# Six tokens of every head on 96 partitions: another layout for k and v of two batches in a fused linear-attention and SwiGLU kernel

## The chip, the cores and the metric

The kernel runs on one core of a Trainium2 chip. The metric is the device time of one execution in microseconds (us). Three timed executions of the kernel before gave 323.48, 323.53 and 322.88 us, so its median is 323.48 us.

A core has a tensor engine (PE, with its weight loads listed apart as PEld), a vector engine (DVE), a scalar engine (ACT), a general engine (POOL, in the code `gpsimd` or `G`), a sync engine (SP) that here only issues transfers, and 16 DMA engines that carry the transfers of all queues. Each engine runs its own instructions in order and waits on semaphores for the others.

## The reference

The inputs are q, k and v of 8 batches, 8 heads, 576 tokens and 64 channels, and the weights of a feed-forward layer. All are float32; the kernel computes its products in bfloat16.

```
phi(x) = concat(relu(x) * cos(theta_s), relu(x) * sin(theta_s))    # 64 -> 128 features, theta_s = pi/2 * s/576
kv  = einsum('bhsf,bhsd->bhfd', phi(k), v)        # per batch and head 128 x 64, a sum over the 576 tokens
z   = sum over s of phi(k)                         # 128
num = phi(q) @ kv ;  den = phi(q) @ z + 1e-6
x   = num / den, heads side by side                # 4608 tokens x 512
xn  = x / sqrt(mean(x^2) + 1e-6) * rms_g
out = (silu(xn @ w_gate) * (xn @ w_val)) @ w_out   # 512 -> 1536 -> 512
```

kv and z of a head are one product here: v gets a 65th column of ones, and phi(k) (128 features, stationary) times that v (65 columns, moving) is accumulated over chunks of tokens into one 128 x 65 piece of the PSUM tile `psA`.

## The kernel before

**How the work is tiled.** The feed-forward part works on nine blocks: block b holds 512 tokens of batch b, and block 8 holds the last 64 tokens of all batches. In each block 12 steps make the hidden tile `hT` (gate product, value product, silu on ACT, multiplication on DVE), and four output steps multiply it with `w_out` and store. The attention of batch b + 1 is put between the steps of block b and the first steps of block b + 1, so that PE always has a large product to run. The order of all instructions is written out by hand: `at(block, step, where, function, ...)` (line 753) files small pieces of work into slots, and `run` (line 756) emits them. Nothing reorders them afterwards.

**k and v, and how a batch comes in.** For the sum over tokens any assignment of tokens to partitions is allowed, as long as k, v and the cos/sin table agree. Two layouts are in use before.

- Batches 0, 1 and 2 are narrow: two heads share the 128 partitions, 64 partitions each, and a partition holds 9 consecutive tokens of one head in each of 4 head pairs. `kv_rows` (line 70) describes it; a load has 512 pieces of 2,304 bytes. Each product has 64 rows: the even head on partitions 0 to 63 and the odd head on 64 to 127, so one batch takes 4 pairs x 9 chunks x 2 = 72 products (line 394).
- Batches 3 to 7 are wide (`wide`, line 75): a partition holds 5 consecutive tokens of every head, on 116 partitions (576 = 5 x 115 + 1). A load has pieces of 1,280 bytes and goes in two parts, 112 partitions and the rest. One batch takes 8 heads x 5 chunks = 40 products of 115 or 116 rows (line 387).

A batch needs, in order: the loads of k and v into buffers of a ring (tag `raw`, 5 buffers), `k_phi` (cos half on DVE, sin half on ACT, one instruction for each chunk and half), `v_cast` (to bfloat16 beside the column of ones), `kvz_pe` (the products), `kvz_evac` (ACT copies psA to SBUF), and then four times `nd_pe` and `nd_post` (phi(q) times kv, and the division).

**The start and its POOL queue.** Batch 0 has no large products to hide behind. SP loads its k at once. POOL first writes the token indices with five `iota` instructions (lines 158 to 162; 20 columns of indices, from which DVE and ACT make the cos/sin table `tab`), then issues through its own DMA queue, in this order: half of q of batch 0, v of batch 0 (cast on the way into a tile of its own, `vv0`, line 210), the rest of q, four loads of gate and value weights, k of batch 1 (line 228), gate weights for steps 8 to 11, and later, between other POOL work, value weights for steps 8 to 11, q of batch 1, v of batch 1 (line 699), three loads of `w_out`, k of batch 2 and v of batch 2 (lines 772 and 775). Two POOL memsets at lines 274 and 275 set the columns of ones of two tiles, `vv` for narrow batches and `vv5` for wide ones.

**Batches 1 and 2.** `k_phi` of batch 1 follows units 5, 6 and 7 of block 0, three chunks at a time (line 762). Its `v_cast` is split: POOL casts the first two head pairs (line 773, at step 9) and DVE the last two (line 774, at step 10). POOL issues v of batch 2 behind its cast. `kvz_pe(1)` stands in `last_step` (line 801), between the gate and the value product of step 11. `k_phi` of batch 2 is spread 3, 2, 2 and 2 chunks over four places (line 824, `KCS`), its cast runs on DVE in two halves, and `kvz_pe(2)` comes before step 3 of block 1 (line 839).

Of the kernel before, what the change touches and what calls it, by code (L numbers as in the profile page):

```python
# [9 lines left out]
FP32 = mybir.dt.float32  # L10
# [7 lines left out]
def kernel(  # L18
# [15 lines left out]
    P = 128  # L34
# [3 lines left out]
    NC5 = 5  # L38
    KP = S // NC5 + 1
    KM = 112  # L40
    NDT = DM // P
    NNT = DFF // P
    E = D + 1
# [26 lines left out]
    def kv_rows(src, b, hps):  # L70
        return src[b, 2 * hps[0] : 2 * hps[1], :, :].rearrange(
            "(hp hh) (s c) d -> (hh s) hp (c d)", hh=2, c=NC
        )

    def wide(b):
        return b > 2

    def rows_of(c):
        return KP if c == 0 else KP - 1

    def kv_rows5(src, b, r0, r1):
# [9 lines left out]

    def raw_tile(which, b):
        if (which, b) not in raw:
            t = ring.tile([P, H * NC5 * D], FP32, name="raw", tag="raw")
            raw[(which, b)] = t
        return raw[(which, b)]

    def raw_kv(which, b):
        t = raw_tile(which, b)
        if wide(b):  # L100
            return t[:, :].rearrange("p (h e) -> p h e", h=H)
        return t[:, 0 : HP * NC * D].rearrange("p (hp e) -> p hp e", hp=HP)

    def raw_q(b):
# [2 lines left out]
    def load_kv(which, b, hps=(0, HP), eng=nc.sync):  # L107
        src = k if which == "k" else v
        if not wide(b):
            return eng.dma_start(  # L110
                out=raw_kv(which, b)[:, hps[0] : hps[1], :], in_=kv_rows(src, b, hps)
            )
        last = KP if b < B - 1 else KP - 1
        for r0, r1 in ((0, KM), (KM, last)):
            eng.dma_start(
                out=raw_kv(which, b)[r0:r1, :, :], in_=kv_rows5(src, b, r0, r1)
            )
        if last < KP:
            eng.dma_start(
                out=raw_kv(which, b)[last:KP, :, :].rearrange("p h (c d) -> p h c d", d=D),  # L120
                in_=src[b, :, S - 1 : S, :].rearrange("h s d -> s h d").unsqueeze(2)
                .to_broadcast([1, H, NC5, D]),
            )
# [29 lines left out]
        )  # L153


    NTAB = 20
    idx_i = one.tile([P, NTAB], mybir.dt.int32, name="idx_i")
    G.iota(idx_i[:, 0:9], pattern=[[1, 9]], base=0, channel_multiplier=9)
    G.iota(idx_i[:, 9:13], pattern=[[1, 4]], base=0, channel_multiplier=4)
    G.iota(idx_i[:, 13:14], pattern=[[0, 1]], base=512, channel_multiplier=1)  # L160
    G.iota(idx_i[:, 14:19], pattern=[[1, NC5]], base=0, channel_multiplier=NC5)
    G.iota(idx_i[:, 19:NTAB], pattern=[[0, 1]], base=NC - 1, channel_multiplier=NC)
    warm = one.tile([P, TB], BF16, name="warm")
    V.memset(warm[:, :], 0.0)
    ones = one.tile([P, P], BF16, name="ones")
# [22 lines left out]
    def load_wo(n0, n1):  # L188
        return G.dma_start(
            out=wo[:, n0:n1, :],  # L190
            in_=moe_w_out[n0 * P : n1 * P, :].rearrange("(t p) m -> p t m", p=P),
        )
# [14 lines left out]
                )  # L207
                rest = gres[:, i, :]

    vv0 = one.tile([P, HP, NC * D], BF16, name="vv0")  # L210
    load_q0(0, G)
    for hp in range(0, HP, 2):
        G.dma_start(out=vv0[:, hp : hp + 2, :], in_=kv_rows(v, 0, (hp, hp + 2)))
# [30 lines left out]
        out=th[:, 0:NTAB], in0=fidx[:, :], scalar1=S - 1.0, scalar2=ang,  # L244
        op0=ALU.min, op1=ALU.mult,
    )
    for c0, c1, i0, less in ((0, 9, 0, 576.0), (13, 14, 13, 64.0), (19, NTAB, 13, 64.0)):
        V.tensor_scalar(
            out=th[64:128, c0:c1], in0=fidx[64:128, i0 : i0 + c1 - c0],
            scalar1=-less, scalar2=ang,  # L250
            op0=ALU.add, op1=ALU.mult,
        )
# [12 lines left out]
    def cos_of(c):  # L265
        return tab[:, NTAB + c : NTAB + c + 1]

    kp5 = one.tile([P, NC5, H, F], BF16, name="kp")
    kp = kp5[:, :, :, :].rearrange("p c h f -> p (c h f)")[:, 0 : NC * HP * F].rearrange(
        "p (c hp f) -> p c hp f", c=NC, f=F  # L270
    )
    vv = one.tile([P, HP, NC, E], BF16, name="vv")
    vv5 = one.tile([P, H, NC5, E], BF16, name="vv5")
    G.memset(vv[:, :, :, D:E], 1.0)
    G.memset(vv5[:, :, :, D:E], 1.0)
    qpT = one.tile([P, H, TB], BF16, name="qpT")
    xnT = [one.tile([P, NDT, TB], BF16, name=f"xnT{i}") for i in range(2)]
    xnT_tail = one.tile([P, NDT, TB], BF16, name="xnT_tail")
# [5 lines left out]
    def copy(eng, o, i):  # L284
        if eng is A:
            A.copy(out=o, in_=i)  # L286
        else:
            eng.tensor_copy(out=o, in_=i)  # L288

    def phi(eng, out_ap, in_ap, scale):  # L290
        if eng is A:
            A.activation(out=out_ap, in_=in_ap, func=AF.Relu, scale=scale)  # L292
        else:
            eng.tensor_scalar(  # L294
                out=out_ap, in0=in_ap, scalar1=scale, scalar2=0.0, op0=ALU.mult, op1=ALU.max
            )


    def k_phi(eng, b, c, part, hps=(0, HP)):
        o = slice(0, D) if part == 0 else slice(D, F)  # L300
        f = cos_of if part == 0 else sin_of
        if wide(b):
            rows = rows_of(c)
            src = raw_kv("k", b)[0:rows, :, c * D : (c + 1) * D]
            phi(eng, kp5[0:rows, c, :, o], src, f(14 + c)[0:rows, :])
            return
        src = raw_kv("k", b)[:, hps[0] : hps[1], c * D : (c + 1) * D]
        phi(eng, kp[:, c, hps[0] : hps[1], o], src, f(c))
# [58 lines left out]
        copy(eng, qpT[:, :, j * P : (j + 1) * P], dst)  # L367

    def v_cast(eng, b, hps=(0, HP)):
        if wide(b):  # L370
            src = raw_kv("v", b).rearrange("p h (c d) -> p h c d", d=D)
            hs = slice(2 * hps[0], 2 * hps[1])
            return copy(eng, vv5[0:KP, hs, :, 0:D], src[0:KP, hs])
        copy(
            eng, vv[:, hps[0] : hps[1], :, 0:D],
            raw_kv("v", b)[:, hps[0] : hps[1], :].rearrange("p hp (c d) -> p hp c d", d=D),
        )

    heads = psA[:, :, 0 : HP * E].rearrange("p g (hp e) -> p g hp e", e=E)
    kvzs = {}  # L380

    def kvz_pe(b):
        for hp in range(HP):
            for c in range(NC5 if wide(b) else 0):
                for g in range(2):
                    h, r = 2 * hp + g, rows_of(c)
                    nc.tensor.matmul(  # L387
                        heads[:, g, hp, :], lhsT=kp5[0:r, c, h, :], rhs=vv5[0:r, h, c, :],
                        start=(c == 0), stop=(c == NC5 - 1),
                    )  # L390
            for c in range(0 if wide(b) else NC):
                for g in range(2):
                    lo, hi = 64 * g, 64 * g + 64
                    nc.tensor.matmul(  # L394
                        heads[:, g, hp, :], lhsT=kp[lo:hi, c, hp, :], rhs=vv[lo:hi, hp, c, :],
                        start=(c == 0), stop=(c == NC - 1),
                    )


# [111 lines left out]
    def x_sq(b, j):  # L511
        xt = x_of[(b, j)]
        scr = one.tile([P, DM + 1], BF16, name="scr", tag="scr")
        ms = four.tile([P, 1], FP32, name="ms", tag="ms")
        A.activation(  # L515
            out=scr[:, :], in_=xt[:, 0 : DM + 1], func=AF.Square,
            scale=1.0 / math.sqrt(DM), accum_out=ms[:, :],
        )
        rs = four.tile([P, 1], FP32, name="rs", tag="rs")
        G.tensor_tensor(out=rs[:, :], in0=ms[:, :], in1=mhalf[:, :], op=ALU.pow)  # L520
        rs_of[(b, j)] = rs
# [191 lines left out]
    x_tr_evac(V, 0, 1, psC[0])  # L713
    unit_mm(0, wv)
    x_sq(0, 2)
    load_wo(0, 4)
    unit_silu(0)
    nd0_pe(3)
# [34 lines left out]
    def at(blk, n, where, f, *args):  # L753
        slots.setdefault((blk, n), {}).setdefault(where, []).append((f, args))
# [2 lines left out]
        for f, args in slots.get((blk, n), {}).get(where, []):  # L757
            f(*args)

    KCS = ((0, 1, 2), (3, 4), (5, 6), (7, 8))  # L760
    KCS5 = ((0, 1), (2,), (3,), (4,))
    for c in range(NC):
        at(0, 5 + c // 3, "post", k_phi, V, 1, c, 0)
        at(0, 5 + c // 3, "post", k_phi, A, 1, c, 1)
    for j in range(4):
        at(0, (8, 8, 9, 10)[j], "post", q_phi, V, 1, j, 0)
        at(0, (8, 9, 10, 10)[j], "post", q_phi, A, 1, j, 1)
# [53 lines left out]
    for nb in range(2, B):  # L821
        b = nb - 1
        first = nb == 2
        for i, cs in enumerate(KCS5 if wide(nb) else KCS):
            kb, kn = ((0, 14), (0, 15), (1, 0), (1, 1))[i] if first else (b - 1, 12 + i)
            for c in cs:
                at(kb, kn, "post", k_phi, V, nb, c, 0)
                at(kb, kn, "post", k_phi, A, nb, c, 1)
        for i in range(2):
            vb, vn = ((0, 15), (1, 0))[i] if first else (b - 1, 13 + 2 * i)  # L830
            at(vb, vn, "post", v_cast, V, nb, (2 * i, 2 * i + 2))
        for j in range(4):
            late = j + (nb == 3)
            qb, qn = (b, 1 + j) if first else (b - (late < 2), (14 + late) % 16)
            at(qb, qn, "post", q_phi, V, nb, j, 0)
            at(qb, qn, "post", q_phi, A, nb, j, 1)
            at(qb, qn, "post", q_tr_dma, nb, j)
        kz = 3 if first else 2
        at(b, kz, "pe", kvz_pe, nb)
        at(b, kz, "pre", kvz_evac, A, nb)  # L840
        for j in range(4):
            n = ((6, 8, 9, 11) if first else (4, 6, 8, 10))[j]
            at(b, n, "mid" if n == 9 else "pe", nd_pe, nb, j)
            at(b, n, "pre", nd_post, nb, j)
            at(b, n, "post", x_sq, nb, j)
            m = n + 2 if first and j == 0 else n + 1
            at(b, m, "post", x_norm, nb, j)
            at(b, m, "post", x_tr_dma, nb, j)
# [110 lines left out]
```

## Time and profile before

| | us |
|---|---|
| timed executions | 322.88, 323.48, 323.53 |
| median | 323.48 |
| span of the profiled execution, first to last instruction | 321.1 |
| PE busy | 313.6 (98% of the span) |
| DVE busy | 185.4 (58%) |
| ACT busy | 165.8 (52%) |
| POOL busy | 40.5 (13%) |

The profiled execution gives its span only; its own time would lie above that by what the runtime adds before the first and after the last instruction. Against the median of the timed executions that is 323.48 - 321.1 = 2.4 us. The granted clock of PE is 1.000 over the whole span.

A busy time is the sum of an engine's instructions. The chain of waits follows the instruction that ended last back to what released it, step by step; what is on it sets the time, what is off it does not. A DMA share above 1 in a stretch means that on average more transfers were under way than the 16 engines can carry at once.

### The profile page before, as it was taken

The numbers are of one execution on the slowest core, as the hardware profiler recorded it, in microseconds if no ns is written. First come the engines' busy times: TensorE is split into PE (matmuls) and PEld (weight loads), VectorE is DVE, ScalarE is ACT, GpSimd is POOL, SyncE is SP. The second block draws the span as 40 slices with busy tenths as digits, with TensorE's granted clock in tenths as the row PEclk, the third lists the DMA queues.
The fourth block names the chain that finished last, engine by engine and source line by source line (L and its number), as shares of the span: only waits on it lengthen the run. The fifth ranks groups of instructions, "written<-read, shape, count | busy, mean of one in ns | idle before, by whom it ended". The sixth has DMA issues, their size and how long they took to land.

```text
span 321.1 us, 6023 instructions
## 1 busy us (share of the span) xinstructions
PE 313.6 (98%) x2274; PEld 162.4 (51%) x2310; DVE 185.4 (58%) x382; ACT 165.8 (52%) x322; POOL 40.5 (13%) x79
## 2 busy tenths in 40 slices
PE   7999999999999999999999999999999999999996
PEld 2689564544454445444544445544544444444444
DVE  7976977668457773777457644781676034204410
ACT  5766756754574466554744575446543233223321
POOL 9771211002001100010001100100011000000000
PEclk9999999999999999999999999999999999999999
DMA  7999999788999999999799959995522500041002
GB/s 232 239 270 269 282 329 227 201 183 190 223 226 211 187 263 187 221 247 182 162 186 230 197 163 200 197 217 163 99 59 41 116 33 0 0 102 31 1 35 98
DMA packets 80092, 53.76 MB, mean 167 GB/s; under 512 B 52235, under 2 KB 74047, under 8 KB 80063
## 3 DMA queue, kind: packets, MB, share of 16 engines
q1 hardware_dynamic: 73110, 41.25, 62.1%
q0 software_dynamic: 6944, 12.13, 15.5%
q8 instruction: 18, 0.29, 0.4%
q14 instruction: 12, 0.09, 0.1%
q10 hardware_dynamic: 8, 0.00, 0.0%
HBM read 37.83 MB, written 9.44 MB: 147 GB/s over the span
## 4 chain that ended last, share of the span: by engine, by line
PE 94%; DMA 2%; DVE 1%; issue 1%; POOL 1%; ACT 0%; POOLq 0%; ACTq 0%
PE psC L574 27%; PE psV L556 27%; PE psG L556 26%; PE psV L643 2%; PE psA L449 2%; DMA vv<-in_v_dram 2%; PE psG L574 2%; PE psG L643 2%; PE psA L387 2%; PE psA L394 1%; PE psA L474 0%; PE psV L363 0%; PE psG L430 0%; PE psC L546 0%; POOL raw L135 0%
## 5 line engine op out<-in xcount | busy, mean ns | idle before, releaser
L571 DVE TENSOR_TENSOR hT<-psV,sg 128x512 bf16<-128x512 f32 x99 | 68.2, 689 | 96.5 <-PE psV L556 64.1
L556 PE MATMUL psV<-xnT,wv 128*128 128x512 bf16 x344 | 89.6, 379 | 0.7 <-issue 0.2
L570 ACT ACTIVATE sg<-psG 128x512 f32<-128x512 f32 x99 | 58.6, 592 | 60.8 <-PE psG L556 52.7
L556 PE MATMUL psG<-xnT,wg 128*128 128x512 bf16 x337 | 88.5, 379 | 0.7 <-issue 0.2
L574 PE MATMUL psC<-wo,hT 128*128 128x512 bf16 (+1 forms) x400 | 88.4, 376 | 0.4
L574 PEld LDWEIGHTS <-hT 128*128 128x128 bf16 x456 | 43.1, 98 | 47.7
L556 PEld LDWEIGHTS <-wv 128*128 128x128 bf16 x400 | 39.0, 98 | 46.8
L556 PEld LDWEIGHTS <-wg 128*128 128x128 bf16 x400 | 37.0, 98 | 39.9 <-DVE xnT L288 0.2
L520 POOL TENSOR_TENSOR rs<-ms,mhalf 128x1 f32<-128x1 f32 x36 | 20.5, 570 | 193.9 <-ACT scr L515 193.7
L286 ACT COPY osb<-psC 128x512 f32<-128x512 f32 x32 | 18.7, 585 | 49.9 <-PE psC L574 46.1
L515 ACT ACTIVATE scr<-xt 128x513 bf16<-128x513 f32 x36 | 22.8, 635 | 23.3 <-DVE xt L499 22.3
L527 DVE SCALAR_TENSOR_TENSOR xn<-xt,rs,gb 128x512 bf16<-128x512 f32 (+1 forms) x37 | 26.9, 730 | 9.9 <-POOL rs L520 9.9
L292 ACT ACTIVATE kp<-raw,tab 128x256 bf16<-128x256 f32 (+2 forms) x51 | 28.8, 607 | 2.4 <-DMA raw<-in_k_dram 2.4
L499 DVE TENSOR_TENSOR xt<-psA,rec 128x512 f32<-128x512 f32 x36 | 24.9, 691 | 1.2
L292 ACT ACTIVATE qp<-raw,tab 128x512 bf16<-128x512 f32 (+1 forms) x36 | 23.3, 666 | 1.2 <-DMA raw<-in_q_dram 1.1
L294 DVE TENSOR_SCALAR kp<-raw,tab 128x256 bf16<-128x256 f32 (+2 forms) x53 | 20.1, 428 | 0.5 <-DMA raw<-in_k_dram 0.5
L294 DVE TENSOR_SCALAR qp<-raw,tab 128x512 bf16<-128x512 f32 (+1 forms) x34 | 15.3, 463 | 4.7 <-DMA raw<-in_q_dram 4.7
L449 PEld LDWEIGHTS <-qpT 128*128 128x128 bf16 x224 | 10.6, 97 | 6.6
L556 PE MATMUL psV<-xnT_tail,wv 128*128 128x512 bf16 x48 | 12.3, 379 | 0.1
L556 PE MATMUL psG<-xnT_tail,wg 128*128 128x512 bf16 x46 | 12.0, 379 | 0.1
L288 DVE CAST vv<-raw 116x1280 bf16<-116x1280 f32 (+1 forms) x13 | 11.1, 857 | 1.3 <-DMA raw<-in_v_dram 1.3
L449 PE MATMUL psA<-kvzs,qpT 128*128 128x65 bf16 x224 | 11.4, 193 | 0.0
(102 smaller groups left out, 177.7 us busy)
## 6 DMA issues: line engine op xcount, KB each, us to landing
out_dram<-osb SPq DMA_DIRECT2D x27, 256.0 KB, 2.3
raw<-in_q_dram SPq DMA_DIRECT2D x6, 1024.0 KB, 9.1
raw<-in_k_dram SPq DMA_DIRECT2D x5, 1120.0 KB, 8.8
raw<-in_v_dram SPq DMA_DIRECT2D x5, 1120.0 KB, 9.4
raw<-in_k_dram POOLq DMA_DIRECT2D x2, 1152.0 KB, 19.2
raw<-in_v_dram POOLq DMA_DIRECT2D x2, 1152.0 KB, 15.7
out_dram<-osb SPq DMA_DIRECT2D x17, 128.0 KB, 2.6
wg<-in_moe_w_gate_dram POOLq DMA_DIRECT2D x3, 512.0 KB, 13.8
```

Of the source, the lines that this page charges most:

```text
L286: A.copy(out=o, in_=i)
L292: A.activation(out=out_ap, in_=in_ap, func=AF.Relu, scale=scale)
L294: eng.tensor_scalar(out=out_ap, in0=in_ap, scalar1=scale, scalar2=0.0, op0=ALU.mult, op1=ALU.max)
L449: nc.tensor.matmul(heads[:, g, hp, :], lhsT=qpT[:, h, j * P : (j + 1) * P], rhs=kvzs[b][:, g, hp * E : (hp + 1) * E], start=True, stop=True,)
L499: V.tensor_tensor(out=xt[:, 0:DM].rearrange("p (hp g d) -> p g hp d", g=2, d=D), in0=heads[:, :, :, 0:D], in1=rec[:, :, :].unsqueeze(3).to ...
L515: A.activation(out=scr[:, :], in_=xt[:, 0 : DM + 1], func=AF.Square, scale=1.0 / math.sqrt(DM), accum_out=ms[:, :],)
L520: G.tensor_tensor(out=rs[:, :], in0=ms[:, :], in1=mhalf[:, :], op=ALU.pow)
L527: V.scalar_tensor_tensor(out=xn_of[(b, j)][:, c], in0=x_of[(b, j)][:, c], scalar=rs_of[(b, j)][:, :], in1=gb[:, c], op0=ALU.mult, op1=ALU. ...
L556: nc.tensor.matmul(bank[:, cols[0] : cols[1]], lhsT=w[:, t, n * P : (n + 1) * P], rhs=x[:, t, cols[0] : cols[1]], start=(t == 0), stop=(t ...
L570: A.activation(out=sg[:, :], in_=g[:, 0:TB], func=AF.Silu)
L571: V.tensor_tensor(out=hT[:, n, :], in0=v[:, 0:TB], in1=sg[:, :], op=ALU.mult)
L574: nc.tensor.matmul(bank[:, 0 : cols[1] - cols[0]], lhsT=hT[:, n, j * P : (j + 1) * P], rhs=wo[:, n, cols[0] : cols[1]], start=(n == 0), st ...
```

## The change

Batches 1 and 2 get a third layout: six consecutive tokens of every head on each of 96 partitions (576 = 6 x 96). k and v are one load each, on the same queue and at the same place as before, with 768 pieces of 1,536 bytes. Every head's products have 96 rows and 6 chunks, so a batch takes 8 x 6 = 48 products. `k_phi` and `v_cast` work on 96 partitions, with 512 elements in place of 256 for one chunk, and 1,536 in place of 1,152 for half of v. Batch 0 stays narrow, batches 3 to 7 keep their five tokens.

Around this, the index table grows by six columns and one `iota`, the tiles `raw`, `kp5` and `vv5` get room for six chunks, `vv` goes, `vv0` becomes a view of the memory of `vv5`, and the two memsets of ones become one, which comes later in POOL's queue (behind the third root-mean-square, ahead of the first load of `w_out`) because batch 0 must be done with that memory first. The chunks of `k_phi` are spread 2, 2, 2 for batch 1 and 2, 2, 1, 1 for batch 2.

```
     def wide(b):
-        return b > 2
-    def rows_of(c):
+        return b > 0
+    def chunks(b):
+        return NC6 if b < 3 else NC5
+    def rows_of(b, c):
+        if b < 3:
+            return KP6
         return KP if c == 0 else KP - 1
...
+        if b < 3:
+            return eng.dma_start(
+                out=raw_kv(which, b)[0:KP6, :, :],
+                in_=src[b].rearrange("h (p c) d -> p h (c d)", c=NC6),
+            )
...
-    NTAB = 20
+    NTAB = 26
...
+    G.iota(idx_i[:, 20:NTAB], pattern=[[1, NC6]], base=0, channel_multiplier=NC6)
...
-    vv0 = one.tile([P, HP, NC * D], BF16, name="vv0")
+    vv5 = one.tile([P, H, NC6, E], BF16, name="vv5")
+    vv0 = vv5[:, :, :, :].rearrange("p h c e -> p (h c e)")[:, 0 : HP * NC * D].rearrange(
+        "p (hp e) -> p hp e", hp=HP
+    )
...
-    vv = one.tile([P, HP, NC, E], BF16, name="vv")
-    vv5 = one.tile([P, H, NC5, E], BF16, name="vv5")
-    G.memset(vv[:, :, :, D:E], 1.0)
-    G.memset(vv5[:, :, :, D:E], 1.0)
...
-            rows = rows_of(c)
+            rows = rows_of(b, c)
             src = raw_kv("k", b)[0:rows, :, c * D : (c + 1) * D]
-            phi(eng, kp5[0:rows, c, :, o], src, f(14 + c)[0:rows, :])
+            phi(eng, kp5[0:rows, c, :, o], src, f((20 if b < 3 else 14) + c)[0:rows, :])
...
+        rows, n = KP6 if b < 3 else KP, chunks(b)
+        copy(eng, vv5[0:rows, hs, 0:n, 0:D], src[0:rows, hs])
...
-            for c in range(NC5 if wide(b) else 0):
+            for c in range(chunks(b)):
                 for g in range(2):
-                    h, r = 2 * hp + g, rows_of(c)
+                    h, r = 2 * hp + g, rows_of(b, c)
                     nc.tensor.matmul(
                         heads[:, g, hp, :], lhsT=kp5[0:r, c, h, :], rhs=vv5[0:r, h, c, :],
-                        start=(c == 0), stop=(c == NC5 - 1),
-                    )
-            for c in range(0 if wide(b) else NC):
-                for g in range(2):
-                    lo, hi = 64 * g, 64 * g + 64
-                    nc.tensor.matmul(
-                        heads[:, g, hp, :], lhsT=kp[lo:hi, c, hp, :], rhs=vv[lo:hi, hp, c, :],
-                        start=(c == 0), stop=(c == NC - 1),
+                        start=(c == 0), stop=(c == chunks(b) - 1),
                     )
...
     x_sq(0, 2)
+    G.memset(vv5[:, :, :, D:E], 1.0)
     load_wo(0, 4)
...
-    KCS = ((0, 1, 2), (3, 4), (5, 6), (7, 8))
+    KCS6 = ((0, 1), (2, 3), (4,), (5,))
-    for c in range(NC):
-        at(0, 5 + c // 3, "post", k_phi, V, 1, c, 0)
+    for c in range(NC6):
+        at(0, 5 + c // 2, "post", k_phi, V, 1, c, 0)
...
-        for i, cs in enumerate(KCS5 if wide(nb) else KCS):
+        for i, cs in enumerate(KCS6 if first else KCS5):
```

More of the change, by code (lines that the diff above doesn't have):

```diff
@@ L40 @@
     KM = 112
+    NC6 = 6
+    KP6 = S // NC6
     NDT = DM // P
@@ L93, in raw_tile @@
         if (which, b) not in raw:
-            t = ring.tile([P, H * NC5 * D], FP32, name="raw", tag="raw")
+            t = ring.tile([P, H * NC6 * D], FP32, name="raw", tag="raw")
             raw[(which, b)] = t
@@ L100, in raw_kv @@
         if wide(b):
-            return t[:, :].rearrange("p (h e) -> p h e", h=H)
+            return t[:, 0 : H * chunks(b) * D].rearrange("p (h e) -> p h e", h=H)
         return t[:, 0 : HP * NC * D].rearrange("p (hp e) -> p hp e", hp=HP)
@@ L161 @@
     G.iota(idx_i[:, 14:19], pattern=[[1, NC5]], base=0, channel_multiplier=NC5)
-    G.iota(idx_i[:, 19:NTAB], pattern=[[0, 1]], base=NC - 1, channel_multiplier=NC)
+    G.iota(idx_i[:, 19:20], pattern=[[0, 1]], base=NC - 1, channel_multiplier=NC)
+    G.iota(idx_i[:, 20:NTAB], pattern=[[1, NC6]], base=0, channel_multiplier=NC6)
     warm = one.tile([P, TB], BF16, name="warm")
@@ L246 @@
     )
-    for c0, c1, i0, less in ((0, 9, 0, 576.0), (13, 14, 13, 64.0), (19, NTAB, 13, 64.0)):
+    for c0, c1, i0, less in ((0, 9, 0, 576.0), (13, 14, 13, 64.0), (19, 20, 13, 64.0)):
         V.tensor_scalar(
@@ L266, in cos_of @@
         return tab[:, NTAB + c : NTAB + c + 1]
-    kp5 = one.tile([P, NC5, H, F], BF16, name="kp")
+    kp5 = one.tile([P, NC6, H, F], BF16, name="kp")
     kp = kp5[:, :, :, :].rearrange("p c h f -> p (c h f)")[:, 0 : NC * HP * F].rearrange(
@@ L369, in v_cast @@
     def v_cast(eng, b, hps=(0, HP)):
[L370 to L376, printed above, removed]
-        )
+        src = raw_kv("v", b).rearrange("p h (c d) -> p h c d", d=D)
+        hs = slice(2 * hps[0], 2 * hps[1])
+        rows, n = KP6 if b < 3 else KP, chunks(b)
+        copy(eng, vv5[0:rows, hs, 0:n, 0:D], src[0:rows, hs])
     heads = psA[:, :, 0 : HP * E].rearrange("p g (hp e) -> p g hp e", e=E)
@@ L383, in kvz_pe @@
         for hp in range(HP):
-            for c in range(NC5 if wide(b) else 0):
+            for c in range(chunks(b)):
                 for g in range(2):
-                    h, r = 2 * hp + g, rows_of(c)
+                    h, r = 2 * hp + g, rows_of(b, c)
                     nc.tensor.matmul(
                         heads[:, g, hp, :], lhsT=kp5[0:r, c, h, :], rhs=vv5[0:r, h, c, :],
-                        start=(c == 0), stop=(c == NC5 - 1),
-                    )
-            for c in range(0 if wide(b) else NC):
-                for g in range(2):
-                    lo, hi = 64 * g, 64 * g + 64
-                    nc.tensor.matmul(
-                        heads[:, g, hp, :], lhsT=kp[lo:hi, c, hp, :], rhs=vv[lo:hi, hp, c, :],
-                        start=(c == 0), stop=(c == NC - 1),
+                        start=(c == 0), stop=(c == chunks(b) - 1),
                     )
@@ L758, in run @@
             f(*args)
-    KCS = ((0, 1, 2), (3, 4), (5, 6), (7, 8))
+    KCS6 = ((0, 1), (2, 3), (4,), (5,))
     KCS5 = ((0, 1), (2,), (3,), (4,))
-    for c in range(NC):
-        at(0, 5 + c // 3, "post", k_phi, V, 1, c, 0)
-        at(0, 5 + c // 3, "post", k_phi, A, 1, c, 1)
+    for c in range(NC6):
+        at(0, 5 + c // 2, "post", k_phi, V, 1, c, 0)
+        at(0, 5 + c // 2, "post", k_phi, A, 1, c, 1)
     for j in range(4):
```

## The prediction

> **What bounds the kernel now.** First the page: the totals and the chain by engine.
>
> ```profile
> PE 313.6 (98%) x2274; PEld 162.4 (51%) x2310; DVE 185.4 (58%) x382; ACT 165.8 (52%) x322; POOL 40.5 (13%) x79
> PE 94%; DMA 2%; DVE 1%; issue 1%; POOL 1%; ACT 0%; POOLq 0%; ACTq 0%
> ```
>
> PE is the bound: a product more, or a wait of PE, goes straight into the time. An instruction less elsewhere gains nothing. Next the chain in order of time, at the start and around the products that change (start, us, what).
>
> ```profile
> 1.14 0.09 POOL idx_i L161
> 1.23 0.08 POOL idx_i L162
> ...
> 2.01 1.01 POOL raw L135
> 3.02 6.81 DMA vv<-in_v_dram
> ...
> 38.70 0.86 PE psG L556 x4
> 39.56 1.27 PE psA L394 x72
> 40.83 0.16 issue
> 40.99 0.81 PE psV L556 x3
> ...
> 91.13 1.23 PE psA L387 x40
> ```
>
> The chain begins in POOL's iotas, goes through the first load of v and from then on nearly only over PE. PE reaches the narrow products of batch 1 at 39.56. Then who feeds them: the timeline of POOL and DVE.
>
> ```profile
> 37.45 1.15 POOL L288 CAST vv<-raw 128x1152 bf16<-128x1152 f32 x1 [9.66 <-DMA raw<-in_v_dram]
> 38.54 0.98 POOL L110 DMA_DIRECT2D raw<-in_v_dram  x1
> 37.79 1.42 DVE L288 CAST vv<-raw 128x1152 bf16<-128x1152 f32 x1
> ```
>
> v of batch 1 lands at 37.45, and POOL has waited 9.66 for it. The cast ends at 38.60, 0.96 before PE comes. That is all the room there is, and what sets it is a transfer. So the transfers: busy time by stretch (the last three numbers are PE's clock, the share of the 16 DMA engines and GB/s), and packets in three clean stretches: 45.5 to 48 (k and v of batch 2, 128 partitions, POOL's queue), 128.5 to 132 (k of a wide batch, 112 partitions, SP's queue), and 3 to 5 (k of batch 0, 128 partitions, SP's queue).
>
> ```profile
> 16.00:24.00 8.00, 7.79 (x124) 7.12 (x124) 6.17 (x14) 5.33 (x12) 5.82 (x9) 1.00 1.19 270
> 24.00:32.00 8.00, 8.00 (x82) 7.24 (x80) 5.22 (x12) 5.12 (x12) 1.29 (x2) 1.00 1.16 268
> 32.00:37.00 5.00, 4.95 (x32) 2.72 (x32) 4.24 (x11) 4.05 (x8) 0.00 (x0) 1.00 1.08 330
> ```
> ```profile
> DMA packets 230, 0.99 MB, mean 394 GB/s; under 512 B 16, under 2 KB 16, under 8 KB 230
> ```
> ```profile
> DMA packets 729, 0.93 MB, mean 267 GB/s; under 512 B 0, under 2 KB 729, under 8 KB 729
> ```
> ```profile
> DMA packets 675, 0.75 MB, mean 374 GB/s; under 512 B 16, under 2 KB 675, under 8 KB 675
> ```
>
> From 16 to 37 the DMA engines are always full: what takes longer there moves everything behind it. And 112 partitions go at 267 GB/s where 128 go at 374 to 394, on the same queue too. Two other wide loads, at 136.5 to 140 and 163 to 166, show 280 and 291.
>
> **The change part by part.** The sum is made against the profiled span of 321.1; the median of the timed runs, 323.48, lies 2.4 above it, and I add the differences to that.
>
> *Products.* Narrow: 1.27 for 72, and the four products behind take 0.16 + 0.81 = 0.97 where four take 0.86, so the change of row groups costs another 0.11; together 1.38 a batch. Wide: 1.23 / 40 = 0.031 each with nothing lost behind. 48 x 0.031 = 1.48. Each batch +0.10, both +0.2, all on PE. Bounds: +0.1 (the products take nothing less, only half the switch was real) to +0.3.
>
> *The sixth iota.* It stands ahead of POOL's first load on the chain: 0.08 to 0.09 by the two rows above; if the DMA engines and not the issue set when v lands, nothing. I take +0.09. DVE and ACT work on 26 and 52 columns where they had 20 and 40; the table was ready at 2.67 and k landed at 5.04, which hides it; without that cover it were under 0.1.
>
> *Memsets.* Two (0.27 and 0.39) go from 10.9, ahead of a POOL instruction that waits until 12.96 anyway: no gain. The new one of 48 columns (0.27 to 0.39 x 48/40 = 0.47) comes at 20.58 ahead of the first load of w_out. Next behind it is a POOL power that has waited 0.45 for ACT: covered, at worst 0.02. The load is issued later, but its queue is full.
>
> *k_phi.* Three features of 128x256 took DVE 0.87 and ACT 1.29; two q features of 128x512 took 0.87 and 1.32. Batch 1: nothing. Batch 2: on DVE from 54.90 to its last feature 0.87 + 0.95 + 0.69 + 0.48 + 0.95 + 0.68 + 0.48 against 4.69, so 0.41 later, where a half cast goes from 0.75 to 0.95 (116x1280 takes 0.82). It ended at 59.09 and PE came at 59.43, which this change itself makes 0.3 later, and the last chunk is first used ten products on (0.3). Cover 0.5; without it up to 0.4.
>
> *v_cast of batch 1.* POOL took 1.15 for 1,152 columns; 1,536 take 1.53, so it ends 0.38 later, at 38.98. DVE's half took 0.75 alone in batch 2 and 1.42 here: it ended 0.61 behind POOL's. Scaled by 4/3 that is 0.81 behind, at 39.79. PE arrives at 39.56 + 0.09 = 39.65 and wants DVE's half 24 products (0.74) later, at 40.39. So 0.60 is left for a later landing of v. Behind DVE's cast stand a multiplication (0.68), a feature and the copy of a transpose (ended 40.80); the next PE-bound division was at 42.15: free. Behind POOL's cast stands the issue of v of batch 2.
>
> *Four issues on POOL.* 0.76 for 512 pieces, 0.94 for 1,024 (q of batch 1): about +0.09 each, into a queue that is full: nothing.
>
> *The loads.* k and v of batch 1 are 1.18 MB each: at 394 GB/s 2.99. Nothing in before shows 96 partitions on this queue. Lower end: the rate holds, nothing added (no row of k and v is above 394, and PE would not wait less in any case, so there is no gain). Upper end: 128 to 112 partitions took 394 to 280; the same factor again gives 200, 5.9 us, 2.9 a load. The nearest row is the wide one: as here, a partition takes short pieces of eight heads, and the partitions are not 128. At 280 GB/s a load takes 4.2, so 1.2 more. k stands ahead of v in the same full queue, so v of batch 1 lands 2.4 later. Minus 0.60 of room: PE waits 1.8 at the first products of batch 1. q of batch 1, between the two, lands 1.2 later; its first feature on ACT ended at 35.17 and PE wanted it at 35.92, so 0.4 of that wait would already fall there; it is the same time, not more. Gate and value weights and w_out in the same queue shift with PE.
>
> *Batch 2.* k landed at 27.03 + 20.9 = 47.9 and was wanted at 51.10, v at 50.9 and wanted at 55.42. Three and four slow loads in a row make that 3.6 and 4.8 later, PE is 2.1 later: 51.5 against 53.2, 55.7 against 57.5. Covered, up to 2.9 a load.
>
> Sum: 0.2 + 0.09 + 1.8 = 2.1; 323.48 + 2.1 = 325.6.
>
> A rule on the same point: the Trainium skill, "SBUF — State Buffer", section "Door 1: The DMA port swizzle", says that transfers reach SBUF through 16 ports of eight partitions, that partitions 0 to 63 lie on eight of them and 64 to 127 on the other eight. [...] It speaks against this change too, with another size; the 267 to 291 of the wide rows are slower than its even sharing would make 112 partitions.
>
> **The rivals.**
> (a) The load is on time: the pieces still travel packed, as in POOL's queue now, and 96 partitions divide evenly over 16 engines. For: packets of over 2 KB in the 394 row against 1.3 KB in the wide ones. Against: 3 to 5 has short packets too and runs at 374. Only the products and the iota remain: 323.48 + 0.3 = 323.8, not measurably slower. It decides as long as a load loses less than 0.30 (half of the room).
> (b) An uneven landing side: sixteen equal paths share 394 GB/s, 24.6 each, and partitions 0 to 63 keep eight of them. Two thirds of 1.18 MB through 8 x 24.6 = 197 GB/s take 4.0, so 1.0 a load, v 2.0 late, PE waits 1.4: 325.2. (This is the skill's "Door 1" rule, worked with this case's rates.)
> (c) Worse than any row: 200 GB/s, 2.9 a load, v 5.8 late, PE waits 5.2: 323.48 + 0.3 + 5.2 = 329.0. k and v of batch 2 then end behind the point where they are wanted, and PE waits again at about 59.
> (d) Faster: PE's idle time after 16 is a few tenths, and no part shortens PE. Only the spread of runs gives it.
>
> **How the numbers follow.** The forecast (1 to 1.5 lost a load, 325.1 to 326.3) 0.40; (b) and what lies between it and (a), 324.2 to 325.2, 0.22; (a) 0.22; (c) and above the forecast 0.12; (d) 0.04. The likeliest is 325.6. For 8 in 10 the range goes from 323.6, which takes in most of (a), to 327.6, with (c)'s worst left out. A change under 0.2% (0.65 us) can't be told from none here, the three runs being 0.65 apart: (a) counts as same, 0.22; faster 0.05; slower 0.73.
>
> **What would show it.** The wait of POOL's cast for v's transfer longer than 9.66 by about 2.4, and the cast starting near 39.9. PE idle, released by POOL, ahead of the 96-row products, 1.8; the same shift in every later step, none at batch 2. 48 products in 1.48 with four full products in 0.86 behind. Packets of k and v of batch 2 at about 280 GB/s where 394 stood. I am wrong if v still lands near 37.5 to 38 (then it is a), or if the PE wait is at another place: at the q transposes (35.9), at the weights of steps 8 to 11, or at batch 2.

## The result

The changed kernel takes 330.73 us (median of four executions, 329.92 to 331.07) against 323.42 for the kernel before (four executions, 322.88 to 323.53). The ratio is 1.0223, with a 95% interval of 1.0206 to 1.024: slower by 7.3 us. Forecast were 325.6 and a range that ended at 327.6. The direction was right; the size was not, and the time lies outside the range.

The totals and the chain by engine of the changed kernel:

```profile
span 329.3 us, 5914 instructions
PE 315.4 (96%) x2226; PEld 163.0 (49%) x2262; DVE 187.2 (57%) x376; ACT 166.0 (50%) x316; POOL 40.9 (12%) x79
PE 87%; issue 5%; DMA 2%; DVE 2%; POOL 2%; ACT 1%; ACTq 0%; POOLq 0%; DVEq 0%
```

PE is as busy as before, give or take two us, but its share of the chain has fallen from 94% to 87%: PE waits. (The trace has some matmul records missing, so the busy time itself is not the measure.) The waits are in the timelines of PE, ACT and POOL (start, us, engine and line; in brackets the idle time before it and what ended it). The first line is of the kernel before, the others of the changed one:

```profile
34.45 0.72 ACT L292 ACTIVATE qp<-raw,tab 128x512 bf16<-128x512 f32 x1 [0.33 <-DMA raw<-in_q_dram]
```
```profile
38.07 0.72 ACT L304 ACTIVATE qp<-raw,tab 128x512 bf16<-128x512 f32 x1 [3.74 <-DMA raw<-in_q_dram]
38.85 0.62 PE L375 MATMUL psC<-ident,qp 128*128 128x128 bf16 x8 [2.53 <-ACT qp L304]
...
43.48 1.46 POOL L300 CAST vv<-raw 96x1536 bf16<-96x1536 f32 x1 [13.01 <-DMA raw<-in_v_dram]
44.99 1.71 PE L395 MATMUL psA<-vv,kp 96*128 96x65 bf16 x48 [2.48 <-POOL vv L300]
...
61.15 1.02 PE L557 MATMUL psG<-xnT,wg 128*128 128x512 bf16 x3 [1.13 <-ACT kp L304]
```

Three waits of PE that were not there before. q of batch 1 lands 3.6 later (38.07 where ACT began at 34.45), v of batch 1 lands 6.0 later (43.48, before 37.45). The third wait is put down to ACT, which ended at 61.00. The instruction also reads the transposes of batch 1's normalised rows, which go through the DMA engines: the last of them was issued at 55.4 and landed 5.6 later, at 61.0 too. A later run names them.

How far PE is behind, read at the same places of both traces:

| place | before | after | behind |
|---|---|---|---|
| first gate product of block 0 | 17.46 | 17.54 | 0.08 |
| value product of step 9 | 35.05 | 35.30 | 0.25 |
| q transposes of batch 1 | 35.92 | 38.85 | 2.93 |
| products of batch 1 | 39.56 | 44.99 | 5.43 |
| first division product of batch 1 | 41.80 | 47.57 | 5.77 |
| first value product of block 1 | 55.11 | 62.17 | 7.06 |
| products of batch 3 | 91.13 | 98.28 | 7.15 |
| last long output product | 315.51 | 322.61 | 7.10 |

Of this 7.1, 6.8 is lost between 35 and 62 us, and none of it comes back. The profiled spans differ by more, 329.3 - 321.1 = 8.2: from the last copy to the end, where only the output is still being stored, the changed kernel took 3.6 and the kernel before 2.5. The change does not touch that part. The transfers in a stretch that holds nothing but k and v of batch 2 (52 to 55):

```profile
DMA packets 155, 0.68 MB, mean 226 GB/s; under 512 B 8, under 2 KB 8, under 8 KB 155
q0 software_dynamic: 155, 0.68, 104.6%
```

The engines are just as full (104.6% where the stretch of before had 102.9%), the packets are just as large (0.68 MB in 155), but they move 226 GB/s where it was 394. A packet keeps an engine for longer: 104.6% of 16 engines' 3 us, over 155 packets, is 0.32 us each, and 102.9% of their 2.5 us over 230 packets was 0.18.

### The profile page after: what moved, and what is told of

Its sections match the earlier page's. It is cut to its first block, busy times and chain, and to the rows that moved or that the text cites. A ratio compares the mean times of both kernels' runs of the same rounds, so it can differ in the third digit from the quotient of the medians.

```text
span 329.3 us, 5914 instructions
## 1 busy us (share of the span) xinstructions
PE 315.4 (96%) x2226; PEld 163.0 (49%) x2262; DVE 187.2 (57%) x376; ACT 166.0 (50%) x316; POOL 40.9 (12%) x79
## 4 chain that ended last, share of the span: by engine, by line
PE 87%; issue 5%; DMA 2%; DVE 2%; POOL 2%; ACT 1%; ACTq 0%; POOLq 0%; DVEq 0%
PE psC L575 26%; PE psV L557 25%; PE psG L557 24%; PE psA L395 3%; DMA vv<-in_v_dram 2%; PE psG L575 2%; PE psA L450 2%; PE psV L644 1%; PE psG L644 1%; PE psA L475 0%; POOL vv L300 0%; PE psV L375 0%; DVE xt L500 0%; PE psG L431 0%; ACT kp L304 0%
## 5 line engine op out<-in xcount | busy, mean ns | idle before, releaser
L557 PEld LDWEIGHTS <-wv 128*128 128x128 bf16 x400 | 38.9, 98 | 47.0 <-DMA wv<-in_moe_w_val_dram 0.4
L304 ACT ACTIVATE kp<-raw,tab 115x512 bf16<-115x512 f32 (+3 forms) x45 | 29.0, 679 | 3.2 <-DMA raw<-in_k_dram 3.2
L306 DVE TENSOR_SCALAR kp<-raw,tab 115x512 bf16<-115x512 f32 (+3 forms) x47 | 20.2, 471 | 0.8 <-DMA raw<-in_k_dram 0.8
L300 DVE CAST vv<-raw 116x1280 bf16<-116x1280 f32 (+1 forms) x13 | 12.4, 950 | 4.6 <-DMA raw<-in_v_dram 4.6
L395 PE MATMUL psA<-vv,kp 115*128 115x65 bf16 (+1 forms) x296 | 10.3, 193 | 2.5 <-POOL vv L300 2.5
L395 PEld LDWEIGHTS <-kp 115*128 115x128 bf16 (+1 forms) x296 | 10.1, 97 | 4.3 <-issue 2.8
```

Of the source, the lines that this page charges most:

```text
L306: eng.tensor_scalar(out=out_ap, in0=in_ap, scalar1=scale, scalar2=0.0, op0=ALU.mult, op1=ALU.max)
L395: nc.tensor.matmul(heads[:, g, hp, :], lhsT=kp5[0:r, c, h, :], rhs=vv5[0:r, h, c, :], start=(c == 0), stop=(c == chunks(b) - 1),)
L557: nc.tensor.matmul(bank[:, cols[0] : cols[1]], lhsT=w[:, t, n * P : (n + 1) * P], rhs=x[:, t, cols[0] : cols[1]], start=(t == 0), stop=(t ...
```

## The experiments

**Theories.** A, "where it lands": a transfer to 96 partitions makes several DMA engines write through the same path into the memory, and each packet takes longer. B, "short pieces": 1,536-byte pieces of eight heads are slow to read. C, "number of partitions": fewer than 128 is slow, wherever they lie. And a question beside them: are the late loads all of the 7.3?

**Landing on 128 partitions.** Only the landing changes; the rest of the new layout stays (96 rows, 48 products, the iota, the memory of `vv0`).

```
-                out=raw_kv(which, b)[0:KP6, :, :],
-                in_=src[b].rearrange("h (p c) d -> p h (c d)", c=NC6),
+                out=raw_288(which, b)[:, :, :],
+                in_=src[b].rearrange("h s d -> h (s d)").rearrange("h (p e) -> p h e", p=P),
...
             src = raw_kv("k", b)[0:rows, :, c * D : (c + 1) * D]
+            if b < 3:
+                src = raw_288("k", b)[0:rows, :, (c % 4) * D : (c % 4 + 1) * D]
...
+        if b < 3:
+            one_c = raw_288("v", b)[0:rows, hs, 0:D]
+            ap = list(one_c.ap)
+            src = bass.AP(one_c.tensor, one_c.offset, ap[:2] + [[44, n]] + ap[2:])
+            return copy(eng, vv5[0:rows, hs, 0:n, 0:D], src)
```

`raw_288` is the tile of the load seen as eight runs of 288 elements on each of 128 partitions.

> The changed kernel, but k and v of batches 1 and 2 land on 128 partitions, with eight pieces of 1,152 bytes on each, the same bytes from the same queue at the same place; features, casts and products keep their sizes (96 rows, 512 and 1,536 columns) and read what landed, so the values are not those of the reference. Theory 'where it lands' (engines share paths into the memory when 96 partitions are spread over them): packets of k and v fall from 316 ns back to about 190, v of batch 1 lands near 37.5 to 38, no PE wait at the q transposes, at the products or at block 1, and the time is that of before plus the products and the iota: 323.7 to 324.0. Theory 'short pieces of eight heads' (the source side): the pieces are shorter still, so it stays at 330 or above.

Measured: 323.66 against 323.32, ratio 1.0014 (1.0003 to 1.0025). The casts of POOL and DVE, the products (from the chain) and the transfers from 45.5 to 48:

```profile
37.62 1.46 POOL L303 CAST vv<-raw 96x1536 bf16<-96x1536 f32 x1 [9.50 <-DMA raw<-in_v_dram]
37.78 2.12 DVE L303 CAST vv<-raw 96x1536 bf16<-96x1536 f32 x1
```
```profile
39.55 1.47 PE psA L405 x48
41.02 0.86 PE psV L567 x4
```
```profile
DMA packets 231, 1.02 MB, mean 409 GB/s; under 512 B 9, under 2 KB 9, under 8 KB 231
```

v lands where it landed before, no wait of PE is left, and the rate is back, with pieces of 1,152 bytes, shorter than those of the change. So the landing is all of the loss but about 0.3 to 0.4, and B falls as the main cause on this run alone. It also confirms the room: POOL's cast ends at 39.08 and PE comes at 39.55 without a wait. DVE's half ends at 37.78 + 2.12 = 39.90, and PE wants it 24 products (0.74) after 39.55, at 40.29; so 0.39 is left, with v 0.17 later than before.

**One long piece for each partition.** The opposite test of B: 96 partitions, but one run of 12,288 bytes for each.

```
-                out=raw_kv(which, b)[0:KP6, :, :],
-                in_=src[b].rearrange("h (p c) d -> p h (c d)", c=NC6),
+                out=raw_tile(which, b)[0:KP6, :],
+                in_=src[b].rearrange("h s d -> (h s d)").rearrange("(p e) -> p e", p=KP6),
```

> The changed kernel, but each of the 96 partitions gets one run of 12,288 bytes from memory in place of eight pieces of 1,536 (tokens and heads are mixed up, so the values are not those of the reference; sizes are the same). 'Where it lands': nothing changes, about 330.7, packets near 14.6 GB/s for one engine. 'Short pieces': the packets are back at 24 GB/s for one engine and the time is 323.7 to 324.0.

Measured: 329.93 (ratio 1.0207, 1.0175 to 1.0239). The transfers from 49.6 to 51, and POOL's cast:

```profile
DMA packets 31, 0.33 MB, mean 237 GB/s; under 512 B 4, under 2 KB 4, under 8 KB 4
```
```profile
42.15 1.46 POOL L300 CAST vv<-raw 96x1536 bf16<-96x1536 f32 x1 [12.96 <-DMA raw<-in_v_dram]
```

The rate is 237 GB/s where the change has 226, with pieces eight times as long: B is out as the cause of the loss. That the time comes so near 330.7 is in part luck. v of batch 1 landed 4.7 later than before and not 6.0, and PE has no wait at block 1; but from about 44.5 to 48 its clock was a half (the last section), which costs about 1.7 and which the profiled execution of the change does not have.

**Two cuts of the same load.** Partitions 0 to 63 and then 64 to 95; and, in a second kernel with `((32, KP6), (0, 32))` in the loop, 32 to 95 and then 0 to 31.

```
-            return eng.dma_start(
-                out=raw_kv(which, b)[0:KP6, :, :],
-                in_=src[b].rearrange("h (p c) d -> p h (c d)", c=NC6),
-            )
+            for r0, r1 in ((0, 64), (64, KP6)):
+                eng.dma_start(
+                    out=raw_kv(which, b)[r0:r1, :, :],
+                    in_=src[b].rearrange("h (p c) d -> p h (c d)", c=NC6)[r0:r1],
+                )
+            return
```

> The changed kernel with each of the four loads cut in two: partitions 0 to 63, then 64 to 95. Values are right. 'Where it lands', with the pairing that the 128-partition rate and the skill's port map suggest (four consecutive partitions of the first 64 share a path with the four that lie 32 higher): with four partitions to an engine, engines e and e+8 write the same path all the time, so packets of both parts take 330 to 380 ns and the time is that of the changed kernel or worse, 330 to 333. 'Number of partitions' alone (fewer than 128 is slow): the same as the next run, whatever the cut.

> The same cut at another place: partitions 32 to 95, then 0 to 31; again 64 and 32 partitions, values right. 'Where it lands': partitions 32 to 63 and 64 to 95 use sixteen different paths, one for each engine, so two thirds of the bytes go at 190 ns a packet and one third at 330 to 380: a load takes 3.8 in place of 5.1 to 6, v of batch 1 lands 1.6 to 2.2 later than before, PE waits 1 to 1.6, and the time is 325 to 326. 'Number of partitions' alone, or 'short pieces': as the run before it, about 330.

Measured: 332.18 for the first (ratio 1.0281, 1.025 to 1.0312), 329.78 for the second (1.0212, 1.0155 to 1.027). In the first, v of batch 1 landed at 43.45, where the changed kernel has 43.48, and the time lies in A's range. In the second it landed at 41.72, not at 39 to 39.6, and the time missed A's 325 to 326 by four us: cutting at 32 was not the repair that I had worked out. But the cut changes more than the landing. Both kernels have a wait of PE that the changed kernel does not have (the first kernel, then the second):

```profile
26.10 0.54 PE L549 MATMUL psC<-ident,xn 128*128 128x128 bf16 x4 [2.42 <-DVE xn L530]
```
```profile
26.07 0.40 PE L549 MATMUL psC<-ident,xn 128*128 128x128 bf16 x4 [2.43 <-DVE xn L530]
```

These are normalised rows of batch 0. They wait for a power on POOL, which starts at 24.7 (21.92 in the changed kernel), behind the issue of a `w_out` load that itself waited 1.8. Besides, POOL's cast of v took 2.50 in both where the change has 1.46, and behind the products of batch 1 PE ran at half clock for some 3.4 us (the last section), which costs about 1.7. So the two times do not test A by themselves. A stretch of transfers of the second (49 to 51) ran at 292 GB/s, where the first had 212 (50.5 to 52), so the cut does matter to the rate. The next pair has no further issues on POOL.

**64 partitions, low or in the middle.** Only one part is loaded, and features, casts and products use partitions 32 to 63, which both kernels have. All instructions but the four loads are equal; the second kernel has 32:96 where the first has 0:64. (The same rows are cut in the cast and in the products.)

```
-                out=raw_kv(which, b)[0:KP6, :, :],
-                in_=src[b].rearrange("h (p c) d -> p h (c d)", c=NC6),
+                out=raw_kv(which, b)[0:64, :, :],
+                in_=src[b].rearrange("h (p c) d -> p h (c d)", c=NC6)[0:64],
...
-            src = raw_kv("k", b)[0:rows, :, c * D : (c + 1) * D]
+            r0, rows = (32, 64) if b < 3 else (0, rows)
+            src = raw_kv("k", b)[r0:rows, :, c * D : (c + 1) * D]
```

> The changed kernel with only partitions 0 to 63 of the four loads (two thirds of the bytes); features, casts and products use partitions 32 to 63 alone, so a large part of the sums for batches 1 and 2 is left out, and the products have 32 rows. 'Where it lands' (shared paths): packets of 4,608 bytes take 330 to 350 ns, as in the cut run that began with 0 to 63. 'Number of partitions': the same as the next run.

> The same with only partitions 32 to 95: the same bytes and pieces, the same instructions elsewhere. 'Where it lands': packets of 4,608 bytes take 180 to 200 ns, v of batch 1 lands earlier than in the kernel before (a third of the bytes is missing), and no PE wait for it. 'Number of partitions', 'short pieces': packets as in the run before it.

Measured: 329.17 with partitions 0 to 63 (ratio 1.0185, 1.0159 to 1.0212), 324.73 with partitions 32 to 95 (1.0052, 1.0035 to 1.0068). The cast that waits for v and the transfers, first with 0 to 63 (50 to 52), then with 32 to 95 (42.5 to 44):

```profile
41.99 2.24 POOL L300 CAST vv<-raw 32x1536 bf16<-32x1536 f32 x1 [12.99 <-DMA raw<-in_v_dram]
```
```profile
DMA packets 91, 0.39 MB, mean 197 GB/s; under 512 B 4, under 2 KB 4, under 8 KB 91
```
```profile
35.46 1.46 POOL L300 CAST vv<-raw 32x1536 bf16<-32x1536 f32 x1 [8.72 <-DMA raw<-in_v_dram]
```
```profile
DMA packets 138, 0.60 MB, mean 397 GB/s; under 512 B 9, under 2 KB 9, under 8 KB 137
```

The same count of partitions, the same bytes and pieces: 197 against 397 GB/s, a factor of two. C is out, and what counts is which partitions the load writes. (The two kernels also read other rows of k and v; the run with 128 partitions reads all rows at 409, which speaks against those.) A stands as the explanation; that engines share a path into the memory is not seen itself, only that it fits. The Trainium skill, "SBUF — State Buffer", section "Door 1: The DMA port swizzle", says that partitions 0 to 63 lie on eight of sixteen ports, and by its table 32 to 95 touch all sixteen with four each. The trace agrees with that rule, with 197 against 397. The second kernel takes 324.73 - 323.05 = 1.7 us more than the one before. No transfer wait of PE is in it; PE waits 0.4 for a feature of batch 2 on DVE, and the rest is not explained.

**Only one batch slow.** From the kernel with the 128-partition landing, the 96-partition landing comes back for batch 1 alone, then for batch 2 alone (`b == 2`); `k_phi` and `v_cast` read that batch as the changed kernel does.

```
+            if b == 1:
+                return eng.dma_start(
+                    out=raw_kv(which, b)[0:KP6, :, :],
+                    in_=src[b].rearrange("h (p c) d -> p h (c d)", c=NC6),
+                )
```

> The kernel with the 128-partition landing (324), where only k and v of batch 1 land on 96 partitions again, as in the changed kernel (values of batch 2 are not those of the reference). If a slow load costs by the waits seen in the changed kernel: the waits at the q transposes (2.7) and at the products of batch 1 (2.5 and about 0.2 inside them) come back, the one at block 1 (1.3) does not or only in part, since k and v of batch 2 leave the queue early again: 328.9 to 329.6. If the whole of the loss hangs on batch 1: 330.7.

> The other way round: only k and v of batch 2 land on 96 partitions (values of batch 1 are not those of the reference). The prediction called these loads covered up to 2.9 lost a load: 323.7 to 324.0. The rival: packets of v of batch 2, five or six us longer in the queue, stand before the transposes of batch 1's normalised rows, which share the DMA engines; these land 3 or more later than the 54 of before, and block 1 waits for them 2 to 3 us: 325.5 to 327.

Measured: 328.4 for batch 1 (ratio 1.0154, 1.0129 to 1.0179), 326.58 for batch 2 (1.0103, 1.0071 to 1.0134), beside 323.05 for the kernel before. With batch 1 slow, the waits of PE are at the q transposes and at the products, and none is at block 1:

```profile
38.52 0.67 PE L385 MATMUL psC<-ident,qp 128*128 128x128 bf16 x8 [2.24 <-ACT qp L312]
44.34 1.70 PE L410 MATMUL psA<-vv,kp 96*128 96x65 bf16 x48 [0.49 <-POOL vv L308]
```

The time is half a us below what I expected, but the second wait is 0.5 and not 2.5. From 38.9 to 42.3 PE ran at half clock, which costs it about 1.7 between the two waits, so it came later to the second. The landing of v sets when the products start either way: v landed at 42.83, 0.65 before that of the changed kernel, and that is about the half us.

With batch 2 slow, the loads that the prediction called covered cost 3.5 over the kernel before, where the products and the iota alone cost 0.3, and the trace names why, at the first product of block 1:

```profile
56.10 1.02 PE L572 MATMUL psG<-xnT,wg 128*128 128x512 bf16 x3 [2.37 <-DMA xnT<-xn]
```

These are the transposes of batch 1's normalised rows, under way while v of batch 2 is in the same engines: 6.9 from issue to landing, where the kernel before had 4.3 and the run with both batches on 128 partitions 2.8. Without those 0.3 the two cost 5.0 and 3.2, together 8.2, where both at once cost 7.3 - 0.3 = 7.0. In the traces the wait at block 1 is shorter with both batches slow (1.13 against 2.37; the transposes took 5.6 against 6.9); why is not shown. And the medians hold executions with and without a stretch of half clock (the last section), so the 1.2 between the sums is no measure of one thing.

## Why the prediction was wrong in size

The step that failed is the rate of the 96-partition loads, a term of the sum that was taken from the wrong row: 280 GB/s against 226 measured, and v of batch 1 landed 6.0 later where 2.4 was forecast. A second step, "covered" for batch 2, failed as well and for a reason of its own.

- **The rate of the 96-partition loads.** The prediction took 280 GB/s ("The nearest row is the wide one"), so 1.2 lost a load. The trace shows 226 GB/s with full engines, 1.18 MB / 226 = 5.2 us a load where it was 3.0. That is 2.2 lost a load, but v of batch 1, behind two such loads, came 6.0 later, 3.0 a load. This is the upper end that was written down (200 GB/s, 2.9 a load; it had another wait at about 59 too) and that got 0.12. The wide row was near in its pieces and far in its landing, and the runs show that pieces count for little (237 GB/s with one long piece) beside the landing (409 on 128 partitions). (b) had the right kind of cause; its even sharing (1.0 a load) was a third of what came. Where the 1.6 between 2 x 2.2 and 6.0 comes from stays open, and so does the difference to even sharing: unequal parts for the engines on the landing side could be one reason, but how the transfer divides the 96 partitions among the engines was not measured.
- **The room of 0.60 and what a late landing costs**: right. With the landing restored 0.39 of room is left, and v is 0.17 later, together 0.56. With it late, POOL's cast ends at 44.94 and PE starts at 44.99. DVE's half ended 0.81 behind POOL's, as worked out (43.51 + 2.24 = 45.75), and adds a little inside the products (1.71 where 48 alone take 1.47).
- **The q transposes**: right place, wrong size, for the same cause. With 1.2 lost the prediction had 0.4 there; q landed 3.6 later and PE waited 2.53. As written, that part is no addition: both waits together, 2.53 + 2.48 = 5.0 where 1.8 was forecast, are what the landing of v costs.
- **Batch 2 "covered"**: wrong, and not by size alone. Its features and casts were in time, as worked out: DVE cast v at 61.45 without a wait for its transfer. But the step followed only those who wait for k and v of batch 2. It left out what else these loads hold up, the transposes on SP's queue, which go through the same 16 engines. That cost a wait of PE of 1.13 here, and of 2.37 with only batch 2 slow.
- **The products**: right. 1.47 for 48 (1.48 forecast) with four products in 0.86 behind them; 0.1 a batch over the narrow form.
- **The iota**: right, the first gate product is 0.08 later. **Memsets, features, casts**: as costed; POOL's cast took 1.46 (1.53 forecast), two features 0.87 on DVE and about 1.3 on ACT, the memset 0.30, with 0.42 idle left on POOL before its next power.
- **The sum without the loads**: 0.3 forecast, 323.66 - 323.32 = 0.34 measured (0.1 to 0.8 by the interval).

## What to carry to other kernels

A load to fewer than 128 partitions can cost far more than its share of partitions: here 226 GB/s at 96 and 197 at the low 64, but 397 at partitions 32 to 95. Before a layout is changed, ask which partitions it lands on, and take the price from a row with that landing, not from one with the same pieces. And where a queue of transfers is full, a slower load must be followed to everything that shares the DMA engines, other queues' transposes among them, not only to those who read it.

## What was not expected

After some of the longer waits of PE the granted clock fell to a half for a while, though PE was busy again. In the run with only batch 2 slow, the busy time by stretch (PE's clock is the third number from the end):

```profile
53.50:57.00 3.50, 1.08 (x6) 0.46 (x6) 2.35 (x4) 1.22 (x2) 0.00 (x0) 1.00 1.17 257
57.00:57.70 0.70, 0.70 (x4) 0.26 (x3) 0.00 (x0) 0.54 (x2) 0.00 (x0) 0.81 1.11 351
57.70:61.00 3.30, 3.30 (x9) 1.21 (x8) 1.95 (x3) 1.52 (x4) 0.00 (x0) 0.52 1.06 378
61.00:64.00 3.00, 3.00 (x45) 1.92 (x44) 2.25 (x5) 2.16 (x4) 0.00 (x0) 1.00 0.03 12
```

The wait of 2.37 ended at 56.10, and from about 57.5 to 61 the clock was about a half. Three groups of four products took 1.28, 1.71 and 1.29 there, and take 0.86 each at full clock: 1.7 us more. The four executions of this kernel differ in the same way: 327.15 and 327.52 with a mean clock of 0.995, 326.00 and 325.98 with 1.000.

The traces of five other variants show such a stretch of about 3.4 us, each soon after a wait of 1.8 to 3.0. But not every such wait is followed by one: the profiled execution of the changed kernel keeps 1.000 through its waits of 2.53 and 2.48. What decides is not shown. That execution is the slowest of its four, and two of the others have 0.995, so the 7.3 do not hang on this.
